# An angle table in a tile of its own, and two weight folds moved one step earlier, in an FFT + ReGLU kernel

## The chip, the cores and the metric

One NeuronCore of a Trainium2 chip. Times are device microseconds (us) of one execution; each comparison runs the two kernels in alternation on the same chip. Spans read from a profile run from the first to the last instruction and are about 1.8 us shorter than the time of the same execution.

Engines: PE is the TensorE matmul, PEld its weight load, DVE is VectorE, ACT is ScalarE, POOL is GpSimd, SP is SyncE, which here only issues DMAs. L468 is line 468 of the kernel before. The changed kernel has one line more near the top, so the same line is L469 there.

## The reference

```python
# x: (8, 3008, 256) float32; w_gate, w_val: (256, 1536); w_out: (1536, 256)
X = np.fft.fft(x, axis=1)
X = np.fft.fft(X, axis=2)
h = X.real.astype(np.float32).reshape(8 * 3008, 256)
gate = np.maximum(h @ w_gate, 0.0)
out = ((gate * (h @ w_val)) @ w_out).astype(np.float32)
```

## The kernel before

The kernel builds its tables of cosines and sines itself, multiplies the DFT over `dim` into the two weight matrices ("folding" them: `wst` times the table `cd` gives `wc` and `ws`), and runs the DFT over `seq` as products with tables. It works on 8 batches of 3 blocks of 12 steps; a step takes 128 of the 1536 hidden columns. Roughly the first 54 us hold the tables, the first batch's products, the folds and the first block. All after that is limited by PE (busy for 73.00 of the 73.00 us from 127 to 200).

The part with the wait. In the trace of this kernel DVE runs its instructions in the order in which they are written: the bit columns, which need neither `dd` nor `perm`, come behind the multiply of 9.02, from 10.07 on. The engines run beside each other (ACT's copy of 8.20 to 9.09 beside POOL's `perm` of 8.37 to 8.98) and wait where they share a tile: DVE's multiply waits 2.07 us for POOL's `perm`.

```python
# POOL's list ("pl"): index tables and the loads of the first batch
iota(pl, mi[:], ...)                                  # partition number
iota(pl, free(dd[:], ...), ...)                       # column number
load_first(12, 4)                                     # DMA issues: lo, hi
load_first(16, 4)
pl.tensor_scalar(perm[:], dd[:], scalar1=mi[:], scalar2=None, op0=ALU.is_equal)
...
# DVE, ACT and PE
group((1, 2, 3), False)                               # PE: products of the first rows
warm(9)                                               # PE: 9 matmuls of no use but to keep PE busy
...
dve.tensor_scalar(dd[:], dd[:], scalar1=mi[:], scalar2=None, op0=ALU.mult)   # in place
residue(dd[:], dq[:], D, dve)
jj, sl, up, odd = bits(0, 15), bits(4, 1), bits(5, 3), bits(0, 1)
ends(24, 8)                                           # DVE: copies from hi
back(25, 3, "act"); back(28, 3, "dve"); ...
group((1, 2, 3), True)                                # PE: products that need those copies
```

The folds of the weights, and where they are put between the steps:

```python
def fold_w(n, i, cs, ps=None):
    ps = ps or spare("psw")
    for k, w in ((0, wst[i, n, 2]), (1, wst[i, n, 0])):   # float32 matmuls, 64 rows x 512
        nc.tensor.matmul(ps[64*k:64*k+64, :], lhsT=cd[:, cs, 64*k:64*k+64], rhs=w, ...)
    nc.scalar.copy((wc, ws)[cs][i][:, sl_], ps[:])
    if cs and (n or i):
        scale_w(n, i, ps)                             # DVE: wm
...
for n in (1, 2):
    for k, t in enumerate(((1, 2, 2, 3), (4, 5, 6, 7))[n - 1]):
        at(t, fold_w, n, k // 2, k % 2)               # after step t
```

The handover from batch 0 to batch 1, where one row of `pq` goes to DRAM and comes back on all partitions, through the same queue (SP's) that loads batch 2 (`load_x` for the second half also has POOL issue a gather, `xhb`, of about the same size):

```python
# stage2, when cs == 1
nc.sync.dma_start(out=row, in_=pq[0:1, 1, :])                       # Nd <- pq
nc.sync.dma_start(out=nbt[b, blk][:], in_=view(row, 0, [[0, 128], [1, 512]]))   # nb <- Nd
...
for half, k in enumerate((5, 24) if b else (14, 31)):
    at(t0 + k, load_x, b + 2, half, nc.sync)          # 750 KB for the second half
```

`even(t)` on DVE reads `nb` and gives `E`; PE's next use of that PSUM slot waits for it (for 0.85 us in the changed kernel).

Of the kernel before, what the change touches and what calls it, by code (L numbers as in the profile page):

```python
# [11 lines left out]
F32 = mybir.dt.float32  # L12
BF16 = mybir.dt.bfloat16
I32 = mybir.dt.int32
ALU = mybir.AluOpType
# [29 lines left out]
def kernel(ctx: ExitStack, tc, x, w_gate, w_val, w_out, out):  # L45
# [4 lines left out]
    B, S, D = x.shape  # L50
    DF = w_gate.shape[1]
    NA, NB = 94, 32
    H = D // 2
# [138 lines left out]
    def back(r, n, evac):  # L192

        dst = tabs["back"][:, r:r + n, 1:H]
        src = free(xt[0]["lo" if r < NB // 2 else "hi"][0:NA], r % 16 * D + D - 1, [D, n], [-1, H - 1])
        if evac == "act":
            nc.scalar.copy(dst, src)
        else:
            nc.vector.tensor_copy(dst, src)
# [109 lines left out]
    cd = hp.tile([128, 2, 512], F32, tag="h", name="cd")[:, :, 0:H]  # L309
# [38 lines left out]
    with tc.tile_pool(name="sp", bufs=1, space=SB) as sp:  # L348
        dve, pl = nc.vector, nc.gpsimd

        def residue(t, q, n, eng):

            eng.tensor_scalar(q, t, scalar1=1.0 / n, scalar2=RND, op0=ALU.mult, op1=ALU.add)
            eng.tensor_scalar(q, q, scalar1=-RND, scalar2=float(n), op0=ALU.add, op1=ALU.mult)
            eng.tensor_tensor(t, t, q, op=ALU.subtract)

        def sines(out, r, n, sign):
            nc.scalar.activation(out, r, ACTF.Sin, scale=sign * 2.0 * math.pi / n * (1.0 - 2e-7))

        def cosines(out, a, n):  # L360

            nc.scalar.activation(out, a, ACTF.Sin, scale=-2.0 * math.pi / n, bias=qpi[0:a.shape[0], :])

        def absolute(out, a):
            nc.scalar.activation(out, a, ACTF.Abs)
# [11 lines left out]
        tq = sp.tile([NA, J, 48], F32, tag="tq")  # L377
        mi = sp.tile([128, 1], F32, tag="mi")
        dd = sp.tile([128, H], F32, tag="dd")
        dq = sp.tile([128, H], F32, tag="dq")  # L380
        ws0 = sp.tile([128, 1], F32, tag="ws0")
        kbi = sp.tile([128, 4, NB], F32, tag="kbi")
# [50 lines left out]
        def bits(shift, mask):  # L433
            ti = sp.tile([128, 1], I32, tag=f"b{shift}{mask}i")
            dve.tensor_scalar(ti[:], pi[:], scalar1=shift, scalar2=mask,
                              op0=ALU.logical_shift_right, op1=ALU.bitwise_and)
            tf = sp.tile([128, 1], F32, tag=f"b{shift}{mask}f")
            dve.tensor_copy(tf[:], ti[:])
            return tf
# [6 lines left out]
        def group(cs, upper):  # L446
            for k in (0, 1):
                for c in cs:
                    first_products(c, upper, k)
# [15 lines left out]
        nc.scalar.mul(wn[:, 0, 9:16, :], wn[:, 1, 9:16, :], -1.0)  # L465
        nc.scalar.copy(w1[:, 1:10, :], wn[:, 1, 1:10, :])
        back(0, 2, "dve")
        dve.tensor_scalar(dd[:], dd[:], scalar1=mi[:], scalar2=None, op0=ALU.mult)  # L468
        residue(dd[:], dq[:], D, dve)  # L469
        jj, sl, up, odd = bits(0, 15), bits(4, 1), bits(5, 3), bits(0, 1)  # L470

        ends(24, 8)
# [34 lines left out]
        ends(16, 4)  # L507
        back(16, 4, "dve")
        dve.tensor_scalar(tis[:], tis[:], scalar1=NB - 1, scalar2=None, op0=ALU.bitwise_and)
        absolute(dq[:], dd[:])  # L510
        cosines(cd[:, 0, 1:H], dq[:, 1:H], D)
        sines(cd[:, 1, 1:H], dd[:, 1:H], D, 1.0)
        group((6, 7, 0), False)
        first_evac(4, "act")
        nc.sync.dma_start(out=seen[:], in_=t1t[0][0:1, 0, 8:10])
# [11 lines left out]
        for cs in range(2):  # L527
# [7 lines left out]
                         op0=ALU.is_equal, op1=ALU.mult)  # L535
# [205 lines left out]
    def at(t, fn, *args):  # L741
        extra.setdefault(t, []).append(lambda: fn(*args))

    for n in (1, 2):
        for k, t in enumerate(((1, 2, 2, 3), (4, 5, 6, 7))[n - 1]):
            at(t, fold_w, n, k // 2, k % 2)
    for t, blk, cs, e in ((1, 1, 1, "dve"), (4, 1, 0, "dve"), (6, 2, 1, "dve"), (8, 2, 0, "dve")):
        at(t, upright, blk, cs, e)
    at(3, rotate, 0, 4, 8)
    at(7, rotate, 0, 8, NKA)  # L750
# [29 lines left out]
    n = len(steps) // 2  # L780
# [20 lines left out]
    for p in range(NF // 2, n + NF // 2):  # L801
        t = 2 * p
# [56 lines left out]
```

## Time and profile before

| | kernel before |
|---|---|
| time, 4 runs | 628.42 us median (628.23 to 628.81) |
| span of the profiled run | 626.4 us |
| first gate matmul (start of step 0) | 24.49 us |
| first out product (`po`, in step 12) | 53.93 us |
| PE waits after 54 us | 0.2 us in all |

The first 54 us are a stage in which PE has holes; the 572 us after it have next to none. The lines of the profile stand in the prediction.

### The profile page before, as it was taken

To read this page: it belongs to the slowest core of one execution; us is meant where nothing else is said; L and a number is where in the kernel's file an instruction comes from. 1 tells how busy PE (TensorE), PEld (TensorE's weight loads), DVE (VectorE), ACT (ScalarE), POOL (GpSimd) and SP (SyncE) were. 2 spreads that over 40 slices of the span, in tenths; PEclk is the share of its full clock that TensorE was granted. 3 is DMA by queue.
4 is the path that set the end of the run, shared out by engine and by line. 5 is a ranking of instruction groups with operands and counts; after the bars stand their busy time and mean duration, and the time that the engine had idled before them with its cause. 6 is when DMAs were issued, how large, how long until landed. Compare 5 with 4: busy or idle time off the path is not lost.

```text
span 626.4 us, 11966 instructions
## 1 busy us (share of the span) xinstructions
PE 615.6 (98%) x4284; PEld 409.9 (65%) x4284; DVE 537.5 (86%) x654; ACT 444.7 (71%) x855; POOL 520.1 (83%) x447
## 2 busy tenths in 40 slices
PE   7999999999999999999999999999999999999996
PEld 4435666766676666667666666666666666666665
DVE  7577888998889998888988898898988889899991
ACT  6667777776777768777777767777677777766660
POOL 7887998998989998988989989898988865565665
PEclk9999999999999999999999999999999999999999
DMA  7777166614744173712826246541732124212114
GB/s 167 207 154 155 32 168 154 145 36 136 171 107 109 41 214 77 171 40 83 216 59 141 45 151 146 116 106 35 218 83 60 34 84 117 60 34 67 33 35 99
DMA packets 42038, 67.44 MB, mean 108 GB/s; under 512 B 5877, under 2 KB 31774, under 8 KB 39962
## 3 DMA queue, kind: packets, MB, share of 16 engines
q1 hardware_dynamic: 37162, 50.61, 32.5%
q0 software_dynamic: 4656, 15.88, 10.8%
q8 instruction: 33, 0.54, 0.4%
q10 hardware_dynamic: 160, 0.20, 0.1%
q14 instruction: 27, 0.22, 0.1%
HBM read 38.85 MB, written 30.17 MB: 110 GB/s over the span
## 4 chain that ended last, share of the span: by engine, by line
PE 93%; DMA 2%; POOL 2%; DVE 1%; issue 1%; ACT 1%; SPq 0%; POOLq 0%
PE po L682 40%; PE V L633 19%; PE G L618 9%; PE G L619 9%; PE G L625 9%; PE ps L162 2%; DMA xha<-in_x_dram,ix 2%; PE ps L271 2%; PE psw L333 1%; POOL hi L132 0%; DMA wst<-in_moe_w_gate_dram 0%; PE ps L216 0%; DVE h L646 0%; PE psk L397 0%; POOL lo L129 0%
## 5 line engine op out<-in xcount | busy, mean ns | idle before, releaser
L653 POOL TENSOR_TENSOR h<-gm,E 128x992 bf16<-128x992 f32 (+1 forms) x138 | 320.0, 2319 | 82.1 <-DVE E L660 52.7
L682 PE MATMUL po<-wo,h 128*128 128x256 bf16 (+2 forms) x2304 | 328.6, 273 | 0.0
L682 PEld LDWEIGHTS <-h 128*128 128x128 bf16 (+2 forms) x2304 | 231.1, 103 | 106.1
L627 ACT ACTIVATE gm<-G 128x496 f32<-128x496 f32 (+1 forms) x288 | 170.5, 592 | 94.3 <-PE G L625 86.7
L646 DVE TENSOR_TENSOR h<-gs,V 128x1024 bf16<-128x1024 f32 (+3 forms) x150 | 173.8, 1159 | 59.1 <-PE V L633 41.1
L640 DVE SCALAR_TENSOR_TENSOR E<-nb,af,V 128x496 f32<-128x496 bf16 (+1 forms) x276 | 190.2, 731 | 1.3 <-POOL h L653 0.9
L620 ACT ACTIVATE gs<-G 128x497 f32<-128x497 f32 (+2 forms) x288 | 169.7, 589 | 24.8 <-PE G L619 24.8
L660 DVE SCALAR_TENSOR_TENSOR E<-E,V 128x992 f32<-128x992 f32 (+1 forms) x138 | 164.6, 1192 | 0.0
L625 PE MATMUL G<-pq,wm 128*128 128x496 bf16 (+1 forms) x288 | 107.9, 375 | 0.3 <-ACT gs L620 0.3
L618 PE MATMUL G<-pq,wc 128*128 128x497 bf16 (+2 forms) x288 | 108.0, 375 | 0.0
L619 PE MATMUL G<-pq,ws 128*128 128x497 bf16 (+2 forms) x288 | 108.0, 375 | 0.0
L633 PE MATMUL V<-pq,wc 128*128 128x497 bf16 (+2 forms) x288 | 85.4, 375 | 0.0
L633 PE MATMUL V<-pq,ws 128*128 128x497 bf16 (+2 forms) x288 | 85.4, 375 | 0.0
L619 PEld LDWEIGHTS <-ws 128*128 128x128 bf16 x288 | 28.1, 98 | 32.7
L695 ACT COPY os<-po 128x512 f32<-128x512 f32 x63 | 36.9, 586 | 14.7 <-PE po L682 13.2
L633 PEld LDWEIGHTS <-wc 128*128 128x128 bf16 x288 | 28.1, 98 | 20.1 <-issue 1.8
L114 POOL TENSOR_TENSOR eo<-xla 94x256 bf16<-94x256 f32 x56 | 40.2, 730 | 0.7
L618 PEld LDWEIGHTS <-wc 128*128 128x128 bf16 x288 | 28.1, 98 | 18.7 <-DVE pq L278 0.8
L114 POOL TENSOR_TENSOR eo<-xlb 94x256 bf16<-94x256 f32 (+1 forms) x42 | 34.4, 820 | 0.9
L111 POOL TENSOR_TENSOR xla<-xla,xha 94x510 f32<-94x510 f32 x28 | 32.9, 1173 | 2.2
L177 ACT CAST t<-ps 96x512 bf16<-96x512 f32 x56 | 32.7, 583 | 2.4 <-PE ps L162 0.2
L625 PEld LDWEIGHTS <-wm 128*128 128x128 bf16 x288 | 28.1, 98 | 3.3 <-issue 0.8
(142 smaller groups left out, 372.2 us busy)
## 6 DMA issues: line engine op xcount, KB each, us to landing
out_dram<-os SPq DMA_DIRECT2D x124, 128.0 KB
Td<-t SPq DMA_DIRECT2D x7, 768.0 KB
t<-Td SPq DMA_DIRECT2D x7, 768.0 KB
out_dram<-os SPq DMA_DIRECT2D x82, 64.0 KB
xla<-in_x_dram SPq DMA_DIRECT2D x7, 720.0 KB
xlb<-in_x_dram SPq DMA_DIRECT2D x6, 640.0 KB
nb<-Nd SPq DMA_DIRECT2D x23, 128.0 KB
out_dram<-os SPq DMA_DIRECT2D x40, 48.0 KB
```

The source lines that it names most:

```text
L114: yield eng.tensor_tensor(e1[:, :, k:k + H], x1[:, :, 0:H], free(x1, D, [DX, n], [-1, H]), op=op)
L618: nc.tensor.matmul(G[:, ds], lhsT=wc[0][:, fs], rhs=pq[:, 0, ds], start=True, stop=False)
L619: nc.tensor.matmul(G[:, ds], lhsT=ws[0][:, fs], rhs=pq[:, 1, ds], start=False, stop=True)
L620: nc.scalar.activation(pair(t, "gs")[:, t % 2, ds], G[:, ds], ACTF.Relu)
L625: nc.tensor.matmul(G[:, cols], lhsT=wm[0][:, f * 128:(f + 1) * 128], rhs=pqt[b, blk][:, 1, cols], start=False, stop=True, skip_group_check ...
L627: nc.scalar.activation(pair(t, "gm")[:, t % 2, cols], G[:, cols], ACTF.Relu)
L633: nc.tensor.matmul(pair(t, "V")[:, t % 2, cs], lhsT=w[:, f * 128:(f + 1) * 128], rhs=pqt[b, blk][:, min(k, 1), cs], start=(k == 0), stop=( ...
L640: nc.vector.scalar_tensor_tensor(pair(t, "E")[:, t % 2, cols], nbt[b, blk][:, cols], af[:, f:f + 1], pair(t, "V")[:, t % 2, cols], op0=ALU ...
L646: nc.vector.tensor_tensor(pair(t, "h")[:, k, 0, 0:ds.stop - ds.start], pair(t, "gs")[:, k, ds], pair(t, "V")[:, k, ds], op=ALU.mult)
L653: eng.tensor_tensor(free(pair(t, "h")[:], 1024 * (t % 2) + 512 + w - 1, [1024, n], [-1, w]), pair(t, "gm")[:, k, cols], val[:, k, cols], o ...
L660: nc.vector.scalar_tensor_tensor(E[:, :, cols], E[:, :, cols], 2.0, V[:, :, cols], op0=ALU.mult, op1=ALU.subtract)
L682: nc.tensor.matmul(po[0:m, i, :], lhsT=pair(t - f + ff, "h")[:, ff % 2, sg, g * 128:g * 128 + m], rhs=wo[:, ff, :], start=(ff == 0), stop= ...
```

## The change

Its intent: DVE no longer overwrites `dd`, so that it need not wait until POOL has read it for `perm`; and the eight folds that are left for the first block are spread one to a step, from step 0 on. One `upright` (PE transposes of the next block) makes room.

```diff
+        da = sp.tile([128, H], F32, tag="da")
...
-        dve.tensor_scalar(dd[:], dd[:], scalar1=mi[:], scalar2=None, op0=ALU.mult)
-        residue(dd[:], dq[:], D, dve)
+        dve.tensor_scalar(da[:], dd[:], scalar1=mi[:], scalar2=None, op0=ALU.mult)
+        residue(da[:], dq[:], D, dve)
...
-        absolute(dq[:], dd[:])
+        absolute(dq[:], da[:])
         cosines(cd[:, 0, 1:H], dq[:, 1:H], D)
-        sines(cd[:, 1, 1:H], dd[:, 1:H], D, 1.0)
+        sines(cd[:, 1, 1:H], da[:, 1:H], D, 1.0)
...
-        for k, t in enumerate(((1, 2, 2, 3), (4, 5, 6, 7))[n - 1]):
+        for k, t in enumerate(((0, 1, 2, 3), (4, 5, 6, 7))[n - 1]):
             at(t, fold_w, n, k // 2, k % 2)
-    for t, blk, cs, e in ((1, 1, 1, "dve"), (4, 1, 0, "dve"), (6, 2, 1, "dve"), (8, 2, 0, "dve")):
+    for t, blk, cs, e in ((2, 1, 1, "dve"), (4, 1, 0, "dve"), (6, 2, 1, "dve"), (8, 2, 0, "dve")):
         at(t, upright, blk, cs, e)
```

## The prediction

3.0 us for wait and clock and 0.5 for the fold, less 0.1 for stretched instructions, are 3.4 us, and 628.61 - 3.4 = 625.2. Two steps stand as estimates from a few lines: that the half clock goes when the stretch from 9.6 is filled, from one pair of stretches (PE busy for 1.39 of 3.40 us, then clock 0.50 for 3.40 us), and the 0.1, from two instructions of 0.60 and 0.36 us. "Window" means such a stretch of 3.40 us.

> **What bounds the kernel now.** I first read the busy time of each engine by stretch, to see where time can be lost at all.
>
> ```profile
> core 0: us, PE busy (x) PEld busy (x) DVE busy (x) ACT busy (x) POOL busy (x), PEclk, DMA share, GB/s
> 0.00:10.00 10.00, 8.17 (x33) 3.52 (x33) 6.76 (x20) 7.70 (x16) 8.07 (x23) 1.00 0.75 117
> 10.00:20.00 10.00, 8.28 (x64) 6.02 (x64) 6.62 (x37) 5.62 (x15) 8.30 (x15) 0.83 0.55 157
> ...
> 40.00:54.00 14.00, 13.16 (x86) 5.81 (x84) 11.48 (x20) 9.50 (x20) 13.27 (x21) 1.00 0.93 168
> ...
> 127.00:200.00 73.00, 73.00 (x518) 49.87 (x517) 65.10 (x73) 53.84 (x103) 66.46 (x56) 1.00 0.46 114
> ```
>
> From 54 us on PE is busy all the time (73.00 of 73.00), and its waits after 54 us sum to 0.2 us. So an earlier start of the steady part should reach the end unchanged, and only the first 54 us can be changed by this edit. There PE has holes, and between 10 and 20 us its granted clock is 0.83.
>
> The timeline of the first 20 us shows the hole. Columns: start, duration, engine, line, operation, then the idle time before it and what ended it.
>
> ```profile
> 6.32 0.27 POOL L368 IOTA dd<- 128x128 f32 x1
> ...
> 8.37 0.61 POOL L415 TENSOR_SCALAR perm<-dd,mi 128x128 bf16<-128x128 f32 x1
> ...
> 9.02 0.29 DVE L468 TENSOR_SCALAR dd<-dd,mi 128x128 f32<-128x128 f32 x1 [2.07 <-POOL perm L415]
> ...
> 11.28 0.18 DVE L190 COPY hi<-hi 94x8 bf16<-94x8 bf16 x1
> ...
> 11.52 0.67 PE L216 MATMUL ps<-wn,hi 94*128 94x192 bf16 x6 [2.03 <-DVE hi L190]
> ```
>
> DVE wants to multiply dd in place, but POOL still has to read dd for perm, and POOL issues two DMAs first. It is a write-after-read wait, 2.07 us. DVE works in order, so eleven instructions that need no perm, the rest of the angles and the bit columns, stand behind it, then the copies from hi, and PE waits 2.03 us for those.
>
> The hole has a second price. The stretch table cut at the clock's edges:
>
> ```profile
> 9.60:13.00 3.40, 1.39 (x15) 1.24 (x16) 3.05 (x23) 1.33 (x4) 2.19 (x5) 1.00 1.06 253
> 13.00:16.40 3.40, 3.40 (x16) 2.21 (x16) 3.21 (x14) 1.98 (x6) 3.25 (x6) 0.50 0.50 192
> 16.40:19.80 3.40, 3.30 (x37) 2.56 (x34) 0.56 (x1) 2.41 (x7) 3.17 (x6) 1.00 0.14 25
> ```
>
> PE is busy 1.39 of 3.40 us, and in the next 3.40 us its granted clock is 0.50.
>
> [...] the gates start 0.21 to 0.22 us apart (24.49, 24.71, 24.92). [...] The moved work will run beside POOL's DMA issues, so some of it may stretch: a tensor_scalar of 94x384 that met such an issue took 0.60 us at 3.80, another of the same shape 0.36 us at 4.44.
>
> **Part one, the tile of its own (da).** Nothing is added or removed but 512 bytes a partition. The built programs have the same instructions on every engine, and on DVE's order up to the first block nothing moves; the multiply still waits for POOL, but only for the iotas mi and dd, done at 6.59.
> 1. The multiply can start when DVE is free, 6.96 instead of 9.02. From it to the first copy out of hi DVE took 11.07 - 9.02 = 2.05 us, so that copy comes at 9.0 to 9.3. Its data: issued at 3.04, and the transfers of hi land 5.6 to 5.9 us after issue, so 8.9 at the latest. PE followed the copy's start by 0.45, so it goes on at 9.5 to 9.7 instead of 11.52. PE's nine warming matmuls end at 9.49: the hole nearly closes, worth about 2.0 us.
> 2. With the window from 9.6 filled, the half clock of 13.0 to 16.4 should be gone. Four warming matmuls took from 13.85 to 15.56, 1.71 us; at full speed the nine before took 0.21 each, so 0.85.
> 3. The sum of 1 and 2 is capped by loads that do not move:
>
> ```profile
> lo<-in_x_dram POOLq DMA_DIRECT2D x2, 192.0 KB, 5.5
> ...
> hi<-in_x_dram,ixf POOLq DMA_INDIRECT x3, 5.6
> ```
>
> The last lo, issued at 6.51, lands near 12.0; the last hi, issued at 7.37, near 13.0 to 13.3. ACT then runs, in order:
>
> ```profile
> 13.54 0.63 ACT L197 COPY back<-lo 94x508 bf16<-94x508 bf16 x1
> ...
> 14.72 0.29 ACT L358 ACTIVATE cd<-dd 128x127 f32<-128x127 f32 x1
> 16.67 0.91 ACT L230 CAST t<-ps 128x384 bf16<-128x384 f32 x2 [1.65 <-PE ps L216]
> 17.45 0.70 ACT L522 ACTIVATE sv<-tis,npi 128x128 f32<-128x128 int32 x2
> ```
>
> The copy to the end of the sine is 15.01 - 13.54 = 1.47 us, so from 12.05 to 13.5. Half of the pair of evictions adds 0.5: 14.0 to 14.2 instead of 17.2. The products of column pair 0 need that PSUM slot and started at 17.23. PE's own path to there (groups 4, 5, warming, at full speed) gives 13.1 to 13.4, so the load and ACT decide, not PE. Gain at this point: 3.0 us.
> 4. From 17.23 to the first gate at 24.49 there are 7.26 us. I keep them, after looking at each thing that could come late. The first pair of weights lands at 10.04 + 4.3 = 14.3 and DVE folds it in 1.4 us, 15.7, needed at 19.13 - 3.0 = 16.1. POOL's pair for w_val moves less: POOL issues DMAs until 11.72, so its table step moves from 12.92 to 11.75 and its pair ends at 19.44 - 1.17 = 18.3, needed at 22.14 - 3.0 = 19.1. The weights of the second third follow the same eviction through the sync queue: landing 21.8 - 3.0 = 18.8, POOL free at 18.7. Nothing binds, with margins of 0.4 to 0.8 us. The gate starts at about 21.5.
>
> **Part two, the folds.** The same eight folds of wst run, in the same number of matmuls; one upright moves from step 1 to 2. Order: step 0 gets a fold, step 2 loses its second. PE in steps 0 and 1:
>
> ```profile
> 25.25 0.38 PE L633 MATMUL V<-pq,ws 128*128 128x496 bf16 x1
> 25.88 0.37 PE L625 MATMUL G<-pq,wm 128*128 128x496 bf16 x1 [0.25 <-ACT gs L620]
> ...
> 26.62 0.37 PE L633 MATMUL V<-pq,wm 128*128 128x496 bf16 x1
> ```
>
> Starts are 0.63 and 0.32 us apart where 0.21 is the pace: 0.42 + 0.11 = 0.53 us idle, waiting for ACT's first Relu and DVE's wm. A fold of 1.0 us put in front of the 25.88 matmul covers both; later it is not in step 2, where PE had no hole. Gain 0.5 us. It needs POOL's pair, which ended at 24.46 and moves to 21.5; the fold wants it at 21.5 + 1.0 = 22.5, so 1.0 us to spare. The second pair ends at 28.35 - 3.0 = 25.4, wanted in step 2 at about 27.
>
> **Sum.** 3.0 + 0.5 = 3.5 us, less 0.1 for stretched DVE and POOL instructions: 3.4. 628.61 - 3.4 = 625.2 us.
>
> **Rivals.**
> - *The loads eat it.* DMA is saturated there (1.06 of its engines between 9.6 and 13.0), and the landing times are medians of few transfers. If lo or hi lands a microsecond later than worked out, the gain is 2.5: 626.1. [...]
> - *The half clock stays or moves.* [...] 3.4 us at half speed come back, worth 1 us or so where PE is the limit: 626.2. For it: two waits remain in that part. Against: PE is about 80 to 90% busy instead of 41%.
> - *The fold in step 0 becomes a wait.* If PE moves more than POOL's pair, PE stands in front of the fold instead of at the Relu: gain of part two gone or negative by up to 1 us, 625.7 to 626.7. Against: both hang on the same eviction.
> - *Given back later.* POOL's folds of the next batch wait for an indirect load landing at 35.4. If that did not move, the steady part would stop for it. Against: the load stands behind the same weights in the queue and moves with them, and the chunk ready at 41.1 was used first at 54.3.
>
> **Range and chances.** The rivals reach down to gains of about 1.5; a warmer start than worked out, or smaller remaining waits, could give 5. Range 623.4 to 627.2. Two per cent are 12.6 us, more than all idle time of PE in the first 54 us, so neither side of it is likely: within 2% at 0.98.
>
> **What would show it.** The multiply into da at about 7.0 with no wait for perm; PE's hi products near 9.6; granted clock near 1.00 from 13 to 16; column pair 0 at 14.2; first gate at 21.5; in step 0 four half-width fp32 matmuls behind the second V, then mirror gate without wait; step 12's first out product at 50.4 instead of 53.93; the tail unchanged. A gate later than 22.5, a half clock, or a PE wait for POOL's wst would make it wrong.

## The result, and the profile after

The changed kernel takes 625.16 us (median of 4 runs, 624.92 to 625.49) against 628.42 us. The ratio is 0.9948, 95% interval 0.993 to 0.9965. Ratios here are the mean time of one kernel's fast runs over the mean of the other's in the same rounds, so not quite the ratio of the medians. The profiled spans are 623.2 and 626.4 us. The prediction was 625.2 us.

The timeline of the first part of the changed kernel (start, duration, engine, line, operation, count, then idle time before it and what ended it):

```profile
6.63 0.29 DVE L469 TENSOR_SCALAR da<-dd,mi 128x128 f32<-128x128 f32 x1
...
8.39 0.61 POOL L416 TENSOR_SCALAR perm<-dd,mi 128x128 bf16<-128x128 f32 x1
...
9.08 0.18 DVE L190 COPY hi<-hi 94x8 bf16<-94x8 bf16 x1
...
9.32 0.67 PE L216 MATMUL ps<-wn,hi 94*128 94x192 bf16 x6 [0.20 <-DVE hi L190]
...
11.44 0.62 ACT L197 COPY back<-lo 94x508 bf16<-94x508 bf16 x1
...
14.21 0.69 DVE L321 TENSOR_TENSOR wst<-wst 128x512 f32<-128x512 f32 x1 [0.78 <-DMA wst<-in_moe_w_gate_dram]
...
16.04 1.27 POOL L321 TENSOR_TENSOR wst<-wst 128x512 f32<-128x512 f32 x1 [1.01 <-DMA wst<-in_moe_w_val_dram]
```

The multiply now starts at 6.63, 1.76 us before POOL makes `perm`, and has no wait. The copy from `hi` comes at 9.08 instead of 11.28, and PE's idle time ahead of its products is 0.20 us instead of 2.03. The last two lines are new: DVE and POOL now wait for the weights to land.

The stretches of the changed kernel, with the same edges and columns as before (length, busy time and instruction count of PE, PEld, DVE, ACT and POOL, then granted clock, DMA share and GB/s):

```profile
9.60:13.00 3.40, 3.30 (x34) 2.68 (x32) 2.94 (x19) 3.37 (x10) 3.36 (x7) 1.00 1.01 248
13.00:16.40 3.40, 3.30 (x32) 2.29 (x29) 2.55 (x7) 2.67 (x7) 2.19 (x6) 1.00 0.72 237
```

PE is busy for 3.30 instead of 1.39 us of the first stretch, and the half clock of the second is gone.

PE's timeline in steps 0 and 1 of the changed kernel shows the moved fold:

```profile
21.94 0.38 PE L634 MATMUL V<-pq,ws 128*128 128x496 bf16 x1
22.25 1.08 PE L333 MATMUL psw<-wst,cd 128*64 128x512 f32 x4
23.26 0.38 PE L626 MATMUL G<-pq,wm 128*128 128x496 bf16 x1
```

The mirror gate at 23.26 no longer waits for ACT's Relu. Point by point, from the traces of the two kernels and of the two experiments that hold one part each:

| us | before | tile alone | folds alone | after |
|---|---|---|---|---|
| granted clock, 13.0 to 16.4 | 0.50 | 1.00 | 1.00 | 1.00 |
| products of column pair 0 | 17.23 | 14.20 | – | 13.36 |
| first float32 fold | 19.13 | 16.11 | 17.50 | 15.27 |
| first gate | 24.49 | 21.47 | 22.86 | 21.18 |
| first out product | 53.93 | 50.90 | 52.03 | 50.36 |
| gate to out product | 29.44 | 29.43 | 29.17 | 29.18 |
| later PE wait for `nb`, 102 to 107 | 0 | 0.45 | 0.25 | 0.85 |
| span | 626.4 | 623.9 | 625.0 | 623.2 |

After is 3.57 us ahead at the first out product, but only 3.2 at the end. What was given back is in the changed kernel's timeline near the batch handover:

```profile
101.65 1.37 DVE L641 SCALAR_TENSOR_TENSOR E<-nb,af,V 128x496 f32<-128x496 bf16 x2 [1.77 <-PE G L620]
...
103.07 0.58 PE L634 MATMUL V<-pq,ws 128*128 128x496 bf16 x2 [0.85 <-DVE E L641]
```

PE waits 0.85 us for `E`. The releaser that DVE's line names, PE's gate, is only the last semaphore by the profile; what came late is the row `nb`. SP's queue shows it (issue time, time until the issuer goes on):

```profile
89.30 0.97 SPq L93 DMA_DIRECT2D xlb<-in_x_dram  x2
92.76 0.24 SPq L282 DMA_DIRECT2D Nd<-pq  x1
98.68 0.35 SPq L283 DMA_DIRECT2D nb<-Nd  x1
```

`nb` is read from DRAM, so SP waits until the 1 KB row `Nd` has landed before it issues it. That took 98.68 - 92.76 = 5.9 us behind the 750 KB load issued at 89.30.

The row had no slack before the change either. In the kernel before, `nb` was issued at 101.76 and DVE's `E` started 2.97 us later, at 104.73, just in time for PE; in the changed kernel the distance is 2.97 us again (98.68 to 101.65). By then PE's work came 3.96 us earlier than before, but the issue of `nb` only 101.76 - 98.68 = 3.08 us: the difference of 0.88 us is the wait.

**Two levels.** The kernel before has two levels in its runs. Of its 31 runs beside the experiments, 9 took 626.78 to 627.63 us, 20 took 628.2 to 628.94, and 2 took about 630.1. The mean granted clock of the 9 was 0.9978, of the 20 it was 0.9954: (0.9978 - 0.9954) x 627 = 1.5 us of full clock, close to the 1.4 us between the levels' medians (627.20 and 628.59). A half clock of 3.4 us is 1.7 us of the same measure. It doesn't fit every run: 5 of the 20 show 0.997, as high as the lower level. Still, the lower level is probably runs in which no half clock followed the hole in PE. The trace of folds_only below shows such a run (clock 1.00 in both stretches); no trace of the kernel before itself on its low level was taken. Against the high level the change gains 3.3 us, against the low one about 1.8 (627.2 - 625.4).

### The profile page after: what moved, and what is told of

Read it like the earlier page. It is cut to its first block, busy times and chain, and to the rows that moved or that the text cites. A ratio compares the mean times of both kernels' runs of the same rounds, so it can differ in the third digit from the quotient of the medians.

```text
span 623.2 us, 11964 instructions
## 1 busy us (share of the span) xinstructions
PE 614.0 (99%) x4284; PEld 409.6 (66%) x4284; DVE 538.2 (86%) x654; ACT 444.6 (71%) x855; POOL 519.9 (83%) x447
## 4 chain that ended last, share of the span: by engine, by line
PE 96%; DVE 2%; ACT 1%; issue 0%; POOL 0%; POOLq 0%; DVEq 0%
PE po L683 40%; PE V L634 20%; PE G L619 10%; PE G L620 10%; PE G L626 10%; PE psw L333 2%; PE ps L162 2%; PE ps L271 2%; DVE h L647 0%; PE pst L240 0%; PE ps L216 0%; ACT t L230 0%; ACT back L197 0%; PE ps L166 0%; DVE wm L327 0%
```

## The experiments

Eleven runs, two of them the changed kernel again, with runs of the kernel before: chip 13, 628.6 us (626.97 to 628.85); chip 13, 628.32 (626.78 to 628.78); chip 11, 628.58 (627.11 to 630.18). All gave the right result. Theory: the write-after-read wait is worth 3.0 us, half of it its own and half through the clock, the folds less, and a transfer at the handover eats some.

**da_only** and **folds_only**: one part of the change each.

```diff
# da_only: the changed kernel with
-        for k, t in enumerate(((0, 1, 2, 3), (4, 5, 6, 7))[n - 1]):
+        for k, t in enumerate(((1, 2, 2, 3), (4, 5, 6, 7))[n - 1]):
-    for t, blk, cs, e in ((2, 1, 1, "dve"), ...
+    for t, blk, cs, e in ((1, 1, 1, "dve"), ...
# folds_only: the kernel before with the opposite of these four lines
```

> The kernel before with the tile of its own alone, the folds left where they were. My theory (the wait and the half clock are nearly all of the gain): first gate near 21.2 us as in the changed kernel, granted clock 1.00 from 13 to 16.4, time 3.0 us below before (2.7 to 3.3). Rival (the two parts need each other, or the moved folds carry a large share): 2.5 us or less below before. A second rival (what the folds gave is eaten later by the wait for the broadcast row at 102 us anyway): the same time as the changed kernel within 0.15 us.

Measured: 625.66 us (625.62 to 626.16), ratio 0.9962 (0.9948 to 0.9976). In the trace the gate starts at 21.47, 3.02 us earlier than before. The tile alone has nearly the whole gain. By time it can't be told from the changed kernel (625.16, 625.19 and 625.67), so the second rival, that what the folds gave is eaten later, isn't excluded: the folds' share below is shown at the first out product, not at the end.

> The kernel before with the moved folds alone. As put in the prediction: 0.5 us below before, the idle time of 0.53 us in steps 0 and 1. My theory after the trace: only 0.27 us, because two folds in a row cost 0.24 us less than two apart, and step 2 lost its pair. Rival (POOL's pair is late for step 0, ending at 24.46 us against a wish at 25.5): 0 or slower.

Measured: 628.04 us (626.72 to 628.38), ratio 0.9996 (0.998 to 1.0012). By time this says nothing: the runs lie on two levels (626.72 and 626.91; 628.04, 628.26 and 628.38). By trace the folds are worth 29.44 - 29.17 = 0.27 us from gate to out product. The stretches of its profiled run (626.72), cut at the same times, gave something unforeseen:

```profile
9.60:13.00 3.40, 1.55 (x16) 1.21 (x16) 3.03 (x23) 1.78 (x5) 2.19 (x5) 1.00 1.08 237
13.00:16.40 3.40, 3.30 (x33) 2.67 (x33) 3.28 (x15) 3.37 (x10) 3.19 (x7) 1.00 0.59 221
```

The hole is there (1.55 us busy of 3.40), but the clock stays at 1.00. The same hole was followed by a clock of 0.50 in the trace of before (1.39 us busy) and of 1.00 in this one.

**warm_18**: the wait stays, but PE's idle time is filled with more of the useless matmuls. It parts the clock from the wait.

```diff
# the kernel before with
-        warm(9)
+        warm(18)
```

> The kernel before with 18 instead of 9 warming matmuls ahead of the hole, so that PE is busy until 11.4 us while DVE still waits for perm. Theory (the half clock from 13.0 to 16.4 is a price of its own): granted clock 1.00 there, the eviction of column pair 4 at 15.0 instead of 16.67, first gate near 22.9 instead of 24.49, time 1.6 us below before. Rival (only DVE's wait counts, the clock is incidental): within 0.3 us of before.

Measured: 627.27 us (626.95 to 627.55), ratio 0.9986 (0.9972 to 1.0). Its stretches:

```profile
9.60:13.00 3.40, 3.21 (x24) 1.86 (x23) 3.04 (x23) 1.28 (x4) 2.19 (x5) 1.00 1.09 254
13.00:16.40 3.40, 3.30 (x34) 2.67 (x34) 3.27 (x14) 3.37 (x10) 3.19 (x7) 1.00 0.52 192
```

With PE busy for 3.21 of 3.40 us the clock stays at 1.00 in the next stretch, the eviction of column pair 4 starts at 15.01 as expected, and the gate at 22.84: 1.65 us gained by matmuls that compute nothing. This also holds the five runs within 0.6 us, where the kernel before spreads over 1.9. Of the 1.65 us, 1.01 were lost again at the handover, in the same wait for `E`, while the wait at batch 1's turn near 91 us (0.22 us of PE before) is not in this trace's list; the trace's span is 0.9 us shorter (626.4 to 625.5), and the median of the runs is 1.3 us lower than that of before.

**late_load**: the changed kernel, with batch 2's second load put behind the first `Nd` rows.

```diff
-            for half, k in enumerate((5, 24) if b else (14, 31)):
+            for half, k in enumerate((5, 24) if b else (14, 34)):
```

> The changed kernel with the load of the second half of x of batch 2 three steps later (34 instead of 31), out of the way of the row that goes to DRAM and back. Theory (PE's new wait of 0.85 us at 102 us comes from that row standing behind 750 KB of x in the DMA queue): the row lands about 3 us earlier, the wait is gone, 0.85 us below the changed kernel. Rival (the round trip takes 5 us by itself): same as the changed kernel.

Measured: 624.42 us (624.16 to 625.13), ratio 0.9944 (0.9929 to 0.9959). SP's queue in its trace:

```profile
93.27 0.23 SPq L282 DMA_DIRECT2D Nd<-pq  x1
94.36 0.34 SPq L283 DMA_DIRECT2D nb<-Nd  x1
```

With the queue empty the row takes 94.36 - 93.27 = 1.1 us instead of 5.9, and the PE wait for `E` is gone; 0.17 us of wait for a turned tile (`t<-Td`) is all that is left between 85 and 110 us. So the loads of x ahead of the row are the cause of that wait. The edit moves two of them, though: SP's 750 KB and, by the same call, POOL's gather (`xhb`), from 88.50 to 96.74. The next block's row, issued at 97.56 behind the gather but ahead of SP's load, took 100.26 - 97.56 = 2.7 us. So the order in SP's queue is not the whole cause; how the 5.9 us divide between the two loads stays open.

**after_again** and **after_third**: the changed kernel itself, in calls 2 and 3.

> The changed kernel once more, for a comparison on one chip. Theory (the hole is gone[...]): all its runs within 0.6 us of each other, near 625.2 us, while the kernel before falls into two levels, near 628.6 and 627.0, on the same chip. Rival (the two levels belong to something else): the changed kernel shows two levels too.

> The changed kernel a third time, as the measure for the two others of this call: 625.2 us, from 624.5 to 626.2. (The spread of 1.6 us seen the last time was not the clock; I expect it to go with the waits for the turned tile and the broadcast row near 88 and 102 us.)

Measured: 625.19 us (624.53 to 626.15), ratio 0.9954 (0.9942 to 0.9967), and 625.67 us (624.84 to 626.15), ratio 0.9956 (0.994 to 0.9972). The gain repeats, on another chip too. The spread of 1.6 and 1.3 us is wider than I expected of after_again. In three traces of this kernel the wait for `E` was 0.85, 0.16 and 0.35 us and that for `t<-Td` 0, 0.68 and 0.16 us, while the gate started at 21.18, 21.56 and 21.20. So landings of transfers differ from run to run by some tenths; how the spread divides among them stays open.

**pairs**: since two folds in a row had cost PE 1.87 us and a lone one 1.01, I put all of them in pairs.

```diff
# the changed kernel with
-        for k, t in enumerate(((0, 1, 2, 3), (4, 5, 6, 7))[n - 1]):
+        for k, t in enumerate(((0, 0, 2, 2), (4, 4, 6, 6))[n - 1]):
```

> The changed kernel with the folds in pairs, steps 0,0,2,2 and 4,4,6,6. Theory (a fold behind another costs PE 0.24 us less): first out product 0.97 us earlier than in the changed kernel (four pairs), of which the wait for the broadcast row at 102 us takes most: time 0.2 to 0.5 us below the changed kernel. Rival (a pair fills both PSUM slots and waits for their evictions): first out product no earlier.

Measured: 627.86 us (627.4 to 628.22), ratio 0.9996 (0.9983 to 1.0009): 2.7 us slower than after_again. The theory failed. PE's timeline:

```profile
22.77 1.94 PE L333 MATMUL psw<-wst,cd 128*64 128x512 f32 x8
24.64 0.38 PE L626 MATMUL G<-pq,wm 128*128 128x496 bf16 x1
...
39.09 0.37 PE L634 MATMUL V<-pq,wm 128*128 128x496 bf16 x1 [0.74 <-DVE h L647]
```

The pair does cost 24.64 - 22.77 = 1.87 us. But the steps without a fold now wait, for DVE's `h` (four waits, 1.6 us between 27 and 46 us), for its `t` (two, 1.0 us) and for ACT (0.3 us); the changed kernel has one wait there, of 0.17 us. From gate to out product it takes 53.35 - 21.70 = 31.65 us instead of 29.18. A fold in a step is not only PE work; it is also the time in which DVE and ACT catch up. With one fold in each step both are served.

**both_later**: pairs and late_load together.

> The pairs and the later load of x together. If both theories hold the gains add: 0.75 + 0.97 = 1.7 us below the changed kernel, 623.5 us. If the wait at 102 us comes back in another form (the wait for the turned tile from DRAM at 88 us, 0.17 us with the later load): 624.0 to 624.4 us.

Measured: 627.72 us (627.26 to 628.12), ratio 0.9994 (0.9981 to 1.0007). The wait for `E` is gone here too (one of 0.57 us for `t<-Td` stands in its trace), but it stands and falls with pairs; the expectation was missed for the same reason.

**warm_0_after**: the changed kernel without the nine warming matmuls, so that PE has a hole of another cause.

```diff
-        warm(9)
```

> The changed kernel without the nine warming matmuls, so that PE idles from 7.0 to 9.3 us although DVE waits for nothing. Theory (the half clock is set by the idle time[...], whatever caused it): half clock for about 3.4 us in some or most runs, two levels of time, the upper 0.5 to 1.5 us above the changed kernel. Rival (only the wait in DVE's order costs time, the loads bind PE from 9 to 13 us anyway): same as the changed kernel within 0.2 us.

Measured: 627.05 us (626.0 to 628.12), ratio 0.9982 (0.9969 to 0.9996), 1.9 us more than after_again, and more than expected. Its stretches:

```profile
6.20:9.60 3.40, 1.42 (x14) 0.96 (x13) 3.12 (x20) 3.40 (x9) 3.04 (x10) 0.91 1.01 177
9.60:13.00 3.40, 3.40 (x22) 2.87 (x21) 2.52 (x17) 2.58 (x7) 3.36 (x7) 0.50 1.08 235
13.00:16.40 3.40, 3.40 (x22) 2.44 (x21) 1.95 (x6) 1.81 (x7) 1.59 (x5) 0.58 0.57 217
```

The products of `hi` start at 9.37, as in the changed kernel, but PE stood idle 1.81 us before them. Cut finer, the half clock (0.50) runs from 9.0 to 15.8, twice 3.4 us; in the 3.4 us up to 9.0 PE was busy for 1.78. The gate starts at 23.29. No wait of DVE for `perm` is left in this kernel, so here a half clock followed idle time of PE that had another cause. How little PE must be busy for it the runs don't settle: 1.78 and 1.39 of 3.40 us had a half clock behind them (here and in the trace of before), 1.55 in folds_only had none. The time holds more than the clock: in this trace the wait for `E` is 1.23 us. The two levels that I expected are not clear: six runs from 626.0 to 628.12 us, at mean clocks of 0.993 to 0.997.

**perm_early**: the other way to end the write-after-read wait. The multiply stays in place, but POOL makes `perm` before it issues its last loads.

```diff
# the kernel before with
         iota(pl, free(dd[:], 0, [64, 2], [1, 64]), [[1, 2], [2, 64]], 0, 0)
+        pl.tensor_scalar(perm[:], dd[:], scalar1=mi[:], scalar2=None, op0=ALU.is_equal)
         load_first(12, 4)
         load_first(16, 4)
-        pl.tensor_scalar(perm[:], dd[:], scalar1=mi[:], scalar2=None, op0=ALU.is_equal)
```

> The kernel before, in place as it was, with POOL's read of dd for perm moved right behind the iota of dd, ahead of two DMA issues instead of behind them. Theory (nothing but the order of that read made the wait; a tile of its own is one cure of two): DVE's multiply at 7.3 to 7.6 instead of 9.02, clock 1.00, the last loads up to 0.6 us later, time 2.4 to 3.0 us below before, so 0 to 0.6 us above da_only (625.66). Rival (the loads bind hard): the whole 0.6 us and more, 626.3 or above.

Measured: 626.35 us (625.43 to 627.0), ratio 0.9965 (0.9948 to 0.9982). Its timeline:

```profile
7.40 0.29 DVE L468 TENSOR_SCALAR dd<-dd,mi 128x128 f32<-128x128 f32 x1 [0.44 <-POOL perm L413]
...
12.64 0.61 ACT L197 COPY back<-lo 94x508 bf16<-94x508 bf16 x1 [0.56 <-DMA lo<-in_x_dram]
```

The wait shrinks to 0.44 us and the gate comes at 22.06, so the order of `perm` and the multiply was indeed what held DVE. But the last `lo` is now issued at 7.33 instead of 6.51, and ACT waits 0.56 us for it. The rival has a point too: 626.35 lies in the range that it named. By trace the tile of its own is better, since it leaves the loads where they were: its gate comes 22.06 - 21.47 = 0.6 us earlier. By time this isn't shown: the medians lie 0.7 us apart, but on different chips, and the ratios (0.9965 and 0.9962) differ by 0.2 us only, with intervals that overlap.

**best**: late_load, and two smaller moves at the handover.

```diff
# the changed kernel with
+    at(3, rotate, 0, 4, 8)                             # now ahead of the fold in step 3
     for n in (1, 2):
...
-        sh, tr, t2 = (22, 28, (29, 30, 32, 34, 35, 37)) if b else (25, 30, (31, 32, 33, 34, 35, 37))
+        sh, tr, t2 = (22, 28, (29, 30, 32, 34, 35, 37)) if b else (25, 31, (31, 32, 33, 34, 35, 37))
-            for half, k in enumerate((5, 24) if b else (14, 31)):
+            for half, k in enumerate((5, 24) if b else (14, 34)):
```

> The changed kernel with the later load of x (34), the turn of batch 1 at step 31 instead of 30 (its load from DRAM lands late by 0.2 to 0.7 us at 88 us), and in step 3 the turn ahead of the fold (PSUM slot wait of 0.17 us at 32.2 us). If the three waits are separate: 0.75 + 0.2 to 0.7 + 0.17 us below the changed kernel, 623.6 to 624.1 us. Rival (they shift into each other): 624.4 us as with the later load alone.

Measured: 624.67 us (624.25 to 625.59), ratio 0.9939 (0.9922 to 0.9955), 1.0 us below after_third in the same rounds (five of its six runs lie below all six of after_third). The wait for `E` is gone, but the later turn made PE wait 0.44 us for ACT at 89.89: one wait was exchanged for another. late_load with its one number changed reached 624.42. It was run at another time. Against after_third the gain is shown for best as a whole; that late_load alone gives it is argued from the traces, since its interval and after_again's (0.9944 and 0.9954) overlap.

## Why the prediction was right, and where it was off

**The bound.** "From 54 us on PE is busy all the time, so an earlier start should reach the end unchanged" held but for a few tenths. Of 3.57 us at the first out product, 3.2 came to the end: 0.39 were gained on the way and 0.85 lost (see the sum below).

**The wait and the clock (3.0 us).** Both parts were there, and their sum was right. da_only moved the gate by 3.02 us; warm_18 puts 1.65 of it down to the clock, and 22.84 - 21.47 = 1.4 to the wait (the prediction had 2.0 for the wait, before its cap). What decides whether the half clock follows was not shown: the same hole had a clock of 0.50 behind it in the trace of before and of 1.00 in that of folds_only.

**The cap by the loads.** The prediction put column pair 0 at 14.0 to 14.2, behind `lo` and ACT. da_only had it at 14.20, and after at 13.36, because the loads landed faster than in the trace of before, in this trace:

```profile
lo<-in_x_dram POOLq DMA_DIRECT2D x2, 192.0 KB, 5.1
...
hi<-in_x_dram,ixf POOLq DMA_INDIRECT x3, 5.2
```

These are 0.4 us less from issue to landing each (last column). ACT's copy from `lo` then started at 11.44 rather than 12.05. In da_only PE stood 0.40 us in front of column pair 0, waiting for ACT; in this trace it had no wait there, and 13.36 lies in the 13.1 to 13.4 that the prediction gave for PE's own path.

**"Nothing binds, with margins of 0.4 to 0.8 us"** failed in that trace. The 0.8 us that came on top used the margins up: DVE waited 0.78 us for w_gate's weights, POOL 1.01 us for w_val's. From column pair 0 to the gate it took 21.18 - 13.36 = 7.82 us instead of the 7.26 that the prediction kept; in da_only, with 14.20, it took 7.27. So the step was right for the time that it was made for, and of 0.84 us more, 0.56 were lost.

**The moved fold (0.5 us)** is the term of the sum that was mis-sized: 0.26 in after and 0.27 in folds_only. The holes of 0.42 and 0.11 us were filled as foreseen. The failed step is "later it is not in step 2, where PE had no hole", which took for granted that step 2 gives back the fold's full cost. PE's timeline of the kernel before in step 2:

```profile
29.63 0.37 PE L633 MATMUL V<-pq,ws 128*128 128x496 bf16 x1
29.93 1.94 PE L333 MATMUL psw<-wst,cd 128*64 128x512 f32 x8
31.80 0.38 PE L625 MATMUL G<-pq,wm 128*128 128x496 bf16 x1
```

The pair keeps the next gate 31.80 - 29.63 = 2.17 us behind the value matmul. A lone fold in a step of the changed kernel keeps it 25.63 - 24.32 = 1.31 us behind, and no fold 0.21. So a lone fold adds 1.10 us and the second of a pair only 0.86. In step 0 the new fold adds (23.26 - 21.94) - (25.88 - 25.25) = 0.69, step 1 loses its hole of 0.11, and step 2 gives back 0.86: 0.69 - 0.11 - 0.86 = -0.28, close to the 0.26 and 0.27 measured.

**The stretched instructions (0.1 us).** The moved angles and bit columns were not stretched: from the multiply to the first copy out of `hi` DVE took 8.69 - 6.63 = 2.06 us, against 2.05 before. The copy was, in this trace: it took 0.36 us beside POOL's `perm` (8.39 to 9.00), against 0.17 us before. The two lines from which the prediction argued show less than it took from them: the one of 0.36 us at 4.44 also ran beside a DMA issue of POOL's (4.29 to 4.93). The pace of 0.21 us in the sums is the trace's own (gates at 24.49, 24.71 and 24.92).

**The rivals.** The loads did not eat the gain, the half clock did not come back, and the fold in step 0 met no wait. "Given back later" came true in part, elsewhere than I looked: not in POOL's folds of the next batch, but in a 1 KB row behind the loads of x at the handover.

**The sum.** Predicted 3.4 us. Found in the traces: 3.31 us at the gate and 0.26 for the folds make 3.57; at the turn of batch 1's tile, near 88 us, it is 3.96, since PE in the kernel before waited there for `t<-Td` (0.5 us by its weight load) and in this run of the changed kernel did not; less 0.85 at the handover leaves 3.1. The spans differ by 3.2 and the medians by 3.3. Four terms that were each off by 0.24 to 0.85 us (gate, folds, turn, handover) partly cancel, so the closeness of 625.16 to 625.2 owes something to luck, and so does the size of the gain: all 4 runs of the kernel before in this comparison lay on its upper level.

## What to carry to other kernels

When a late engine overwrites a tile in place, look for an earlier reader on an engine that other work holds up: a second tile of 512 bytes a partition was worth 3.0 us at the first gate here, about half of it (1.65 us by warm_18) because the idle PE also lost its clock (0.50 for 3.40 us in the trace of before, 1.00 in that of folds_only), which by their times it probably did in most runs but not in all. Price a moved piece of work by what its old neighbours and its new neighbours make of it, not by its duration alone; a fold cost 1.10 us alone, 0.86 behind another, and as a pair it starved the steps around it. And when a start moves forward, follow the small transfers after it: one of 1 KB behind the loads of x, with no slack left, took back 0.85 of 3.57 us in one trace (0.16 and 0.35 us in two others), and a change of one number in the order of issue removed that wait.
